# Row maxima one step ahead, the row of shifts carried by VectorE transposition and small transfers, and other splits of the keys

## The chip, the cores and the metric

The kernel runs on one core of a Trainium2 chip. A core has five engines that take their own instructions in order and wait for each other by semaphores: TensorE (PE; its weight loads are listed as PEld), VectorE (DVE), ScalarE (ACT), GpSimd (POOL) and SyncE (SP), which issues the transfers here. The metric is device time in microseconds; lower is better.

## The reference

Routed attention, followed by a feed-forward block. A query sees only the keys whose nearest centroid is its own:

```python
batch, n_heads, seq, head_dim = (4, 8, 768, 64);  n_clusters = 16
q_assign = np.argmax(np.einsum('bhsd,hcd->bhsc', q_n, c_n), axis=-1)
k_assign = np.argmax(np.einsum('bhsd,hcd->bhsc', k_n, c_n), axis=-1)
mask = q_assign[:, :, :, None] == k_assign[:, :, None, :]
scores = scale * np.matmul(q, k.transpose(0, 1, 3, 2))
scores = np.where(mask, scores, -1000000000.0)
scores = scores - np.max(scores, axis=-1, keepdims=True)
attn = np.exp(scores)
attn = attn / (np.sum(attn, axis=-1, keepdims=True) + 1e-09)
out = np.matmul(attn, v)
...
h = x @ w_in                       # 3072 tokens, 512 -> 2048
sp = np.maximum(h, 0.0) + np.log1p(np.exp(-np.abs(h)))
g = h * erf(sp)
return g @ w_out                   # 2048 -> 512
```

## The kernel before, in words

The kernel has two stages. The first is attention, some 380 us of the span; the second, the feed-forward block, is not touched. Every engine's instructions of the first stage stand in the order in which the code issues them (`keep_in_program_order`), SP's transfers through `queues[0]` too; the stores to `x_dram` in `divide` are the exception (`nc.sync` directly).

Attention goes by 16 **pairs** of heads. The two heads e = 0, 1 of a pair lie on partitions 0 to 63 and 64 to 127. A pair has two halves of 384 queries and six blocks of 128 keys, so 12 units; a **period** (`period(p, i)`, i = 0 to 5) handles two units: periods 0 to 2 the first half, 3 to 5 the second. The exponentials need a shift for each query, its maximum over the allowed keys, before the half begins, so the maxima of a half are worked out beforehand:

- `maxima_step` forms, for 128 queries (block t) and a part of the keys, the products with queries on the partitions: a first pass over bf16 copies of q and k (`qv`, `kv`) and a second over the rows of the masks (`qm`, `km`), both into the one tile `wide`, which VectorE reduces (`nmx`). TensorE can't write `wide` again before that reduction is done. Each block t has two steps, the first with `KEYS[t]` keys and the second with the rest of the 768.
- Each period has two such steps, half a pair ahead of the scores. The **open step** stands at the period's head, both passes on their own. The **shared step** has its first pass after the period's products q k (`products`, tile `sc`, f32) and its second pass between the two `scores`, which add mask and shift to `sc`; those use 32 of the 64 partitions of each head, the shared step's second pass the other 32.
- When three blocks are through, VectorE takes the smaller of the negated maxima of both parts into `lowest`. At the head of the next period 0 or 3 comes the **turn** (`turn`): six products with `lowest` as weights bring the values into rows of the tile `turned`, and ScalarE copies one row for each head into `qm` (rows 0 and 64), as the row of shifts.

After the scores of a period come, on TensorE: a mask product or the similarities where the period has one; `attend`, 32 products with v for the two units of the period before; and in periods 0 and 3 the sums of `divide`, eight products over the tile that GpSimd has accumulated (`accumulate`, `more_out`). Attend and sums write to `turned`, as similarities and masks do.

The other engines, in the order that the code gives:

- ScalarE: the exponentials (`curve`, two per period, `pr<-sc`), mask copies into `qm` and `km`, logarithm and exponential of the sums (`inv`), and passes over weight strips, which arrive as 64-bit words: in periods 0 and 3 the **sign pass** (`x_own<-x_own`, to int16) behind the two exponentials and ahead of `inv`. In pairs 1 to 14 there is one in period 3.
- VectorE: reductions, 32x32 transpositions (`qT`, `kT`, `sims`, `hotT`, `aside`), in period 0 the copy of the mask into `km`, the division (`den`, then two operations on `turned`, then `x`), two operations on a weight strip.
- GpSimd: in periods 1 and 4 the add that completes a strip (`summed`; the next strip's fetch is issued behind it), then the accumulation of `pr`.

The similarities of pair p + 2 (q and k with the centroids, eight products in the profile) stand in period 3 behind the scores. Of the four mask products for pair p + 1, `MASKS` names period and place: (0, 2) k first half, (2, 3) q first half, (2, 2) k second half, (5, 2) q second half; place 2 is behind the second scores, and its copy on ScalarE stands between the two exponentials except in period 0, where VectorE makes it before the shared step's reduction.

Of the kernel before, what the change touches and what calls it, by code (L numbers as in the profile page):

```python
# [10 lines left out]
BF16 = mybir.dt.bfloat16  # L11
# [16 lines left out]
TW = QW + 1  # L28
HJ = NJ // 2
HP = H // 2  # L30
KEYS = (256, 256, 352, 384, 256, 352)
NPAIR = B * HP
DM, DFF = H * D, 2048
NFT = DFF // P
# [13 lines left out]
N_LATE = 4  # L48
PLACE_OF = [n % 5 for n in range(25)] + [2, 3, 2]
LAST_X = 11  # L50
MASKS = {(0, 2): ("k", 0), (2, 3): ("q", 0), (2, 2): ("k", 1), (5, 2): ("q", 1)}
FIRST_MASKS = {(2, 0): ("k", 0), (2, 1): ("q", 0), (2, 2): ("k", 1), (5, 2): ("q", 1)}

KAPPA = {1: (0, 1), 2: (0, 0), 0: (1, 1), 3: (1, 0)}
HOME = {0: 4, 1: 0, 2: 2, 6: 3, 4: 1, 5: 5}
# [76 lines left out]
def kernel(  # L132
# [55 lines left out]

    lowest = [const.tile([P, HJ, P], BF16, name=f"lowest{i}") for i in range(2)]
    maxima = [const.tile([P, 2, NJ, 3], F32, name=f"nmx{i}") for i in range(2)]  # L190


    lows = [
# [140 lines left out]
    ve.tensor_copy(out=identb, in_=ident)  # L334
    ve.memset(minus, -1.0)
    ve.memset(alleps, S * EPS)
    for t in lowest:
        ge.memset(t, 0.0)

    cn = setup[:, D : 3 * D].rearrange("p (e d) -> p e d", e=2)  # L340
# [104 lines left out]

    turns = []

    def maxima_step(p, i, sm=wide, behind=False):

        st = pairs[p]  # L450
        nmx = maxima[p % 2]
        t, half = divmod(i, 2)

        first = KEYS[t]
        keys = (slice(0, first), slice(first, S))[half]
        n = keys.stop - keys.start

        def passes(a, b, start, rows):
            for e in range(2):
                r = slice(e * D + rows.start, e * D + rows.stop)  # L460
                te.matmul(
                    sm[:, e, 0:n], lhsT=st[a][r, t * P : (t + 1) * P],
                    rhs=st[b][r, keys], start=start, stop=not start,
                )

        passes("qv", "kv", True, slice(0, D))
        if behind:
            yield
        passes("qm", "km", False, slice(Q, D) if behind else slice(0, D))
        if behind:  # L470
            yield
        ve.tensor_reduce(
            out=nmx[:, :, t, half], in_=sm[:, :, 0:n], axis=AX.X, op=ALU.max, negate=True
        )
# [89 lines left out]
    def divide(u):  # L564

        p, half, _ = units[u]
        st = pairs[p]
        av = st["av", half]

        psum = turned[1 - half][:, 0:QW]  # L570
        for g in range(4):
            te.matmul(psum[g * Q : (g + 1) * Q], lhsT=minus, rhs=st["acc", half][:, g], start=True, stop=True)

        if u + 1 < len(units):
            inv = routep.tile([P, QW], F32, name="inv")
            den = routep.tile([P, QW], F32, name="den")
        else:
            inv, den = part_of(0, 4 * HW, QW), part_of(1, 0, QW)
        ae.activation(out=inv, in_=psum, func=ACT.Ln, bias=alleps, scale=-1.0)
        ae.activation(out=inv, in_=inv, func=ACT.Exp, scale=-1.0)  # L580
        yield
        ve.scalar_tensor_tensor(
            out=den, in0=psum, scalar=S * EPS, in1=inv, op0=ALU.subtract, op1=ALU.mult
        )
        for k in range(2):
            raw = av[:, k, 0:QW]
            ve.scalar_tensor_tensor(
                out=raw, in0=raw, scalar=av[:, k, QW : QW + 1], in1=inv, op0=ALU.add, op1=ALU.mult
            )
            if k == 0:  # L590
                yield
        x = part_of(0, (2 * p + half) % 4 * HW, HW).rearrange("p (k x) -> p k x", k=2)
        ve.scalar_tensor_tensor(
            out=x, in0=den.unsqueeze(1).to_broadcast([P, 2, QW]), scalar=2.0, in1=av[:, :, 0:QW],
            op0=ALU.add, op1=ALU.mult,
        )
        b, r = divmod(p, HP)
        for g in range(4):
            rows_of, at = r * P + g // 2 * D, b * S + half * HW + g % 2 * QW
            nc.sync.dma_start(  # L600
                out=x_dram[rows_of : rows_of + D, at : at + QW].rearrange("(k r) x -> r k x", k=2),
                in_=x[g * Q : (g + 1) * Q],
            )
        if half == 1:
            del pairs[p]
        yield
# [725 lines left out]
    def period(p, i):  # L1332
        u = 2 * NJ * p + 2 * i
        n1, n2 = 2 * p - 1, 2 * p
        early = lambda n: 0 <= n < N_EARLY

        def mask(place):
            which = (MASKS if p else FIRST_MASKS).get((i, place))
            if which:
                return masks(p + 1, *which, turned[0 if i in (0, 5) else 1], place == 2, ve if i == 0 else ae)  # L1340
            return lambda: None

        if u > 0:
# [20 lines left out]
        rows = D if u == 0 or u + NJ >= len(units) else Q  # L1364
# [12 lines left out]
        if i == 3:  # L1377
            similarities(p + 2)
            routing[0] = choose(p + 2, turned[0], True)
        curve(u)  # L1380
        later()
        curve(u + 1)
        if u == 0:
            step_ahead(1)
            similarities(1)
            routing[0] = choose(1, turned[0])
            next(routing[0])
            next(routing[0])
            vectors(1, "q")
            vectors(1, "k")  # L1390
        if i == 0 and early(n1 - 1):
            bounded(n1 - 1)
            shifted(n1 - 1)
            sign(n1 - 1)
        elif i == 1 and early(n1):
            size_and_rest(n1)
        elif i == 3 and early(n1):
            sign(n1)
        elif i == 5 and early(n2):
            rest(n2)  # L1400
        for _ in range(min(len(forms), FORMS.get(p, {}).get(i, 0))):
            forms.pop(0)[0]()
        if i == 3:
            next(routing[0], None)
# [79 lines left out]
    for n in range(len(places) - 1):  # L1484
        fetch(n)
    for i in range(NJ):
        run(maxima_step(0, i, also if i % 2 else wide))
# [4 lines left out]
    step_ahead(0)  # L1492
    warm(2, turned[0], zeros)
    turn(0, 0, (ae.copy, ve.tensor_copy))
    turns.clear()
# [111 lines left out]
```

## Time and profile before

| what | us |
|---|---|
| median of 3 runs (953.5 to 954.16) | 953.59 |
| the profiled execution | 953.27 |
| its span | 951.6 |
| TensorE busy in the span | 942.7 (99%) |
| VectorE busy | 789.8 (83%) |
| ScalarE busy | 556.4 (58%) |
| GpSimd busy | 504.3 (53%) |

The profile is of one execution. Nearly every row names line 123, the helper through which instructions are recorded, so rows are told apart by their tiles: `wide` and `nmx` belong to the maxima, `sc` to products and scores, `pr` to the exponentials, `turned<-identb,lowest` to the turn, `turned<-pr,in_v` to attend, `turned<-more_out,minus` to the sums of the division. An f32 product shows as two instructions. Busy times of neighbouring products overlap, and the distance from one start to the next is what a step takes. The steady periods repeat from pair to pair within a few hundredths of a microsecond; the pair from 200 to 224 us, whose period 4 begins at 204.72, stands for all.

### The profile page before, as it was taken

What the parts mean: (1) busy time and instruction counts of PE and PEld (TensorE: products, weight loads), DVE (VectorE), ACT (ScalarE), POOL (GpSimd) and SP (SyncE); (2) the same over time, 40 slices, a digit from 0 to 9 for tenths busy, and PEclk for the clock granted to TensorE, in tenths of its full rate; (3) what the DMA queues carried; (4) which work ended last, traced back from release to release, by engine and by line L of the source; (5) the groups of instructions that cost most, each with busy time, mean ns of one, the idle gap of its engine ahead of it and who ended that gap; (6) DMA issues with size and microseconds to landing.
All of it is one profiled execution on the core that took longest, in us unless ns stands there. A gap on an engine that the chain in (4) does not pass through costs nothing.

```text
span 951.6 us, 22455 instructions
## 1 busy us (share of the span) xinstructions
PE 942.7 (99%) x8938; PEld 719.8 (76%) x8938; DVE 789.8 (83%) x1402; ACT 556.4 (58%) x854; POOL 504.3 (53%) x355
## 2 busy tenths in 40 slices
PE   8999999999999999999999999999999999999998
PEld 3555555555555555588888888998999899989987
DVE  8888888888888887888886688688868977897887
ACT  3777777887777777566513642654257236525541
POOL 1688888888888888899109211360064016103600
PEclk9999999999999999999999999999999999999999
DMA  9355555555454522032786247353444436343533
GB/s 214 73 113 113 113 112 104 120 112 104 103 117 84 132 59 58 18 120 111 199 250 237 101 103 201 127 191 111 155 146 154 133 111 211 111 155 123 155 112 111
DMA packets 175385, 123.14 MB, mean 129 GB/s; under 512 B 131632, under 2 KB 142384, under 8 KB 175280
## 3 DMA queue, kind: packets, MB, share of 16 engines
q1 hardware_dynamic: 170912, 116.29, 43.4%
q0 software_dynamic: 1872, 4.98, 2.9%
q8 instruction: 71, 1.16, 0.5%
q10 hardware_dynamic: 2496, 0.43, 0.2%
q14 instruction: 34, 0.28, 0.1%
HBM read 91.78 MB, written 23.33 MB: 121 GB/s over the span
## 4 chain that ended last, share of the span: by engine, by line
PE 93%; DVE 2%; ACT 1%; issue 1%; DMA 1%; POOL 1%; SPq 0%; DVEq 0%; ACTq 0%; POOLq 0%
PE bank L123 40%; PE turned L123 31%; PE sc L123 17%; PE wide L123 6%; DVE g L123 1%; POOL more_out L123 1%; ACT a_s L123 0%; DMA g_more<-in_moe_w_out_dram 0%; DVE nmx L123 0%; DMA in_k<-in_k_dram 0%; ACT L123 0%; SPq L123 0%; DVE kT L123 0%; ACT osb L123 0%; ACT w_out L123 0%
## 5 line engine op out<-in xcount | busy, mean ns | idle before, releaser
L123 POOL TENSOR_TENSOR more_out<-more_out,pr 128x768 f32<-128x768 f32 x128 | 217.2, 1697 | 15.9 <-ACT pr L123 6.5
L123 DVE TENSOR_REDUCE nmx<-wide 128x2 f32<-128x1024 f32 (+2 forms) x189 | 179.4, 949 | 40.3 <-PE wide L123 39.3
L123 ACT ACTIVATE pr<-sc 128x768 f32<-128x768 f32 x192 | 148.7, 810 | 79.9 <-PE wide L123 66.0
L123 PE MATMUL turned<-pr,in_v 128*32 128x193 f32 x3072 | 144.8, 330 | 0.0
L123 POOL TENSOR_TENSOR g<-g 128x512 f32<-128x512 f32 x36 | 47.2, 1311 | 180.7 <-DVE g L123 178.8
L123 PEld LDWEIGHTS turned<-pr,in_v 128*32 128x32 f32 x3072 | 91.5, 109 | 51.0 <-issue 21.9
L123 DVE TENSOR_TENSOR g<-g 128x512 f32<-128x512 f32 x132 | 90.7, 687 | 22.5 <-PE bank L123 11.4
L123 PE MATMUL sc<-qT,kT 64*128 64x384 f32 x528 | 98.3, 485 | 0.0
L123 DVE TENSOR_TENSOR g<-bank,g 128x256 f32<-128x256 f32 (+1 forms) x128 | 64.6, 530 | 16.1 <-PE bank L123 9.5
L123 PE MATMUL bank<-g_more,g 128*128 128x256 f32 x320 | 75.6, 379 | 0.0
L123 PE MATMUL bank<-x_own,w_in 128*128 128x128 f32 (+1 forms) x440 | 74.0, 310 | 0.0
L123 ACT ACTIVATE a_s<-g 128x1024 f32<-128x1024 f32 x38 | 39.5, 1054 | 56.9 <-POOL g L123 45.3
L123 POOL TENSOR_TENSOR more_out<-pr,pr 128x768 f32<-128x768 f32 x32 | 58.9, 1842 | 20.2 <-ACT pr L123 20.2
L123 DVE TENSOR_TENSOR g<-a_s,g 128x512 f32<-128x512 f32 x76 | 67.3, 904 | 0.4 <-ACT a_s L123 0.4
L123 PEld LDWEIGHTS bank<-g_more,g 128*128 128x128 f32 x320 | 60.8, 190 | 8.3
L123 PEld LDWEIGHTS bank<-x_own,w_in 128*128 128x128 f32 x440 | 63.1, 191 | 4.6 <-issue 0.6
L123 PE MATMUL wide<-kv,qv 64*128 64x512 bf16 (+2 forms) x378 | 64.9, 327 | 1.0 <-ACT km L123 0.6
L123 PE MATMUL bank<-w_out,g 128*128 128x256 f32 x280 | 64.5, 379 | 0.0
L123 PE MATMUL wide<-km,qm 32*128 32x512 bf16 (+2 forms) x378 | 62.4, 326 | 0.0
L123 ACT ACT_TABLE_LOAD x40 | 51.3, 1283 | 18.3 <-DVE g L123 17.7
L123 PEld LDWEIGHTS sc<-qT,kT 64*128 64x128 f32 x528 | 47.8, 187 | 18.6 <-issue 0.9
L123 PEld LDWEIGHTS <-qv 64*128 64x128 bf16 x384 | 24.6, 93 | 47.1 <-issue 29.6
(239 smaller groups left out, 2030.4 us busy)
## 6 DMA issues: line engine op xcount, KB each, us to landing
g_more<-b_dram SPq DMA_DIRECT2D x52, 512.0 KB, 3.3
g_more<-w_dram SPq DMA_DIRECT2D x84, 256.0 KB, 2.9
x_own<-in_moe_w_in_dram SPq DMA_DIRECT2D x13, 512.0 KB, 5.4
in_v<-in_v_dram SPq DMA_DIRECT2D x32, 192.0 KB, 3.2
x_dram<-more_out SPq DMA_DIRECT2D x128, 48.0 KB, 1.7
x_own<-x_dram SPq DMA_DIRECT2D x6, 1024.0 KB, 5.8
in_k<-in_k_dram SPq DMA_DIRECT2D x59, 96.0 KB, 2.8
in_q<-in_q_dram SPq DMA_DIRECT2D x58, 96.0 KB, 5.0
```

What stands on the lines that cost most here:

```text
L123: ins = getattr(self.engine, name)(*args, **kw)
```

## The change

- **Steps.** The maxima run one step further ahead: of the twelve steps of a pair the open places now hold the second parts and the shared places the first parts. `KEYS` becomes 384 for block 0 and 512 for the others, so an open step has 256 keys (384 once) and a shared one 512 (384 once). To get ahead, pair 1's first half is done in five joined steps (`JOINED`) in pair 0's periods 3 to 5; the half before them keeps the old splits.
- **Row of shifts.** For all but pair 0's halves, VectorE reduces into two columns of a tile `least`, transposes its 32x32 blocks into `least_rows`, and four transfers from SP's queue, each of 2 partitions x 3 x 32 values of bf16, bring the rows into `qm`. This is issued right behind the last reduction of the half, an open step's (period 2 for the second half, period 5 for the next pair's first), in place of the turn's six products and two copies.
- **Moves.** From pair 1 on, the similarities of pair p + 2 and the transposition of their result stand at the head of period 3, before the open step. The q mask of the second half goes from place 2 of period 5 to place 2 of period 3. The transposition of k for pair p + 2, with the loads behind it, goes from the end of period 2 to right behind its open step.
- **Stores.** The stores to `x_dram` go a place later and stand in SP's order.

```diff
-KEYS = (256, 256, 352, 384, 256, 352)
+KEYS = (384, 512, 512, 512, 512, 512)
+FIRST_KEYS = (256, 256, 352, 384, 256, 352)
+JOINED = (
+    ((0, 0, 0, 512),), ((0, 1, 512, 768), (1, 0, 0, 256)), ((1, 1, 256, 768),), ((2, 0, 0, 512),), ((2, 1, 512, 768),),
+)
-MASKS = {(0, 2): ("k", 0), (2, 3): ("q", 0), (2, 2): ("k", 1), (5, 2): ("q", 1)}
-FIRST_MASKS = {(2, 0): ("k", 0), (2, 1): ("q", 0), (2, 2): ("k", 1), (5, 2): ("q", 1)}
+MASKS = {(0, 2): ("k", 0), (2, 3): ("q", 0), (2, 2): ("k", 1), (3, 2): ("q", 1)}
+FIRST_MASKS = {(2, 0): ("k", 0), (2, 1): ("q", 0), (2, 2): ("k", 1), (5, 3): ("q", 1)}
...
+    def pieces_of(i, keys_of):
+        t, part = divmod(i, 2)
+        return ((t, part, *((0, keys_of[t]), (keys_of[t], S))[part]),)
+
-    def maxima_step(p, i, sm=wide, behind=False):
+    def maxima_step(p, pieces, sm=wide, behind=False, by_products=False):
...
-        ve.tensor_reduce(
-            out=nmx[:, :, t, half], in_=sm[:, :, 0:n], axis=AX.X, op=ALU.max, negate=True
-        )
-        if i in (NJ - 1, 2 * NJ - 1):
-            h = i // NJ
-            ve.tensor_reduce(
-                out=lowest[h][:, :, ::D].rearrange("p t e -> p e t"),
-                in_=nmx[:, :, h * HJ : (h + 1) * HJ], axis=AX.X, op=ALU.min,
-            )
-            turns.append((p, h))
+        at = 0
+        for t, part, lo, hi in pieces:
+            ve.tensor_reduce(
+                out=nmx[:, :, t, part], in_=sm[:, :, at : at + hi - lo], axis=AX.X, op=ALU.max, negate=True
+            )
+            at += hi - lo
+        h, last = divmod(t, HJ)
+        if part and last == HJ - 1:
+            of_half = nmx[:, :, h * HJ : (h + 1) * HJ]
+            if by_products:
+                ve.tensor_reduce(
+                    out=lowest[h][:, :, ::D].rearrange("p t e -> p e t"), in_=of_half, axis=AX.X, op=ALU.min,
+                )
+                turns.append((p, h))
+            else:
+                into_rows(p, h, of_half)
+
+    def into_rows(p, h, of_half):
+
+        st = pairs[p]
+        ve.tensor_reduce(
+            out=least[h][:, :, 0:2].rearrange("p t e -> p e t"), in_=of_half, axis=AX.X, op=ALU.min
+        )
+        ve.transpose(out=least_rows[h].rearrange("p t q -> p (t q)"), in_=least[h].rearrange("p t q -> p (t q)"))
+        row = st["qm"][::D, h * HW : (h + 1) * HW].rearrange("e (t b q) -> e t b q", t=HJ, q=Q)
+        for b in range(P // Q):
+            queues[0].dma_start(out=row[:, :, b], in_=least_rows[h][b * Q : b * Q + 2])
+        st["shift", h] = True
...
+        yield
         b, r = divmod(p, HP)
         for g in range(4):
...
-            nc.sync.dma_start(
+            queues[0].dma_start(
...
-    def step_ahead(u, behind=False):
-        p, i = divmod(u + NJ, 2 * NJ)
-        steps = maxima_step(p, i, behind=behind) if p < NPAIR else iter(())
+    def step_ahead(p, i, behind=False):
+        if p == 0 and i < NJ:
+            steps = maxima_step(0, pieces_of(NJ + i, FIRST_KEYS), behind=behind, by_products=True)
+        elif p == 0 and i < NJ + len(JOINED):
+            steps = maxima_step(1, JOINED[i - NJ], behind=behind)
+        else:
+            p, i = divmod(2 * NJ * p + NJ + 1 + i, 2 * NJ)
+            steps = maxima_step(p, pieces_of(i, KEYS), behind=behind) if p < NPAIR else iter(())
...
             for which in turns if i in (0, 3) else ():
                 turn(*which)
                 turns.remove(which)
-            step_ahead(u)
+            if i == 3 and p:
+                similarities(p + 2)
+                routing[0] = choose(p + 2, turned[0], True)
+                next(routing[0], None)
+            step_ahead(p, 2 * i)
+            if i == 2:
+                transposes(p + 2, "k")
...
-        second = step_ahead(u + 1, True) if u > 0 else iter(())
+        second = step_ahead(p, 2 * i + 1, True) if u > 0 else iter(())
...
-        if i == 3:
+        if i == 3 and not p:
             similarities(p + 2)
             routing[0] = choose(p + 2, turned[0], True)
...
-        elif i == 2:
-            transposes(p + 2, "k")
```

More of the change, by code (lines that the diff above doesn't have):

```diff
@@ L190 @@
     maxima = [const.tile([P, 2, NJ, 3], F32, name=f"nmx{i}") for i in range(2)]
+    least = [const.tile([P, HJ, Q], BF16, name=f"least{i}") for i in range(2)]
+    least_rows = [const.tile([P, HJ, Q], BF16, name=f"least_rows{i}") for i in range(2)]
     lows = [
@@ L336 @@
     ve.memset(alleps, S * EPS)
-    for t in lowest:
+    for t in lowest + least:
         ge.memset(t, 0.0)
@@ L446 @@
     turns = []
-    def maxima_step(p, i, sm=wide, behind=False):
+    def pieces_of(i, keys_of):
+        t, part = divmod(i, 2)
+        return ((t, part, *((0, keys_of[t]), (keys_of[t], S))[part]),)
+    def maxima_step(p, pieces, sm=wide, behind=False, by_products=False):
         st = pairs[p]
         nmx = maxima[p % 2]
[L452 to L456, printed above, removed]
+        total = sum(hi - lo for _, _, lo, hi in pieces)
         def passes(a, b, start, rows):
[L459 to L463, printed above, removed]
-                )
+            at = 0
+            for t, _, lo, hi in pieces:
+                for e in range(2):
+                    r = slice(e * D + rows.start, e * D + rows.stop)
+                    te.matmul(
+                        sm[:, e, at : at + hi - lo], lhsT=st[a][r, t * P : (t + 1) * P],
+                        rhs=st[b][r, lo:hi], start=start and at == 0, stop=not start and hi - lo + at == total,
+                        skip_group_check=len(pieces) > 1,
+                    )
+                at += hi - lo
         passes("qv", "kv", True, slice(0, D))
@@ L1361, in period @@
         mask(1)()
-        second = step_ahead(u + 1, True) if u > 0 else iter(())
+        second = step_ahead(p, 2 * i + 1, True) if u > 0 else iter(())
         next(second, None)
-        rows = D if u == 0 or u + NJ >= len(units) else Q
+        rows = D if u == 0 or u + NJ + 2 >= len(units) else Q
         scores(u, rows)
@@ L1383, in period @@
         if u == 0:
-            step_ahead(1)
+            step_ahead(0, 1)
             similarities(1)
@@ L1403, in period @@
         if i == 3:
-            next(routing[0], None)
+            if not p:
+                next(routing[0], None)
             if early(n1):
@@ L1486 @@
     for i in range(NJ):
-        run(maxima_step(0, i, also if i % 2 else wide))
+        run(maxima_step(0, pieces_of(i, FIRST_KEYS), also if i % 2 else wide, by_products=True))
         if i == 1:
@@ L1491 @@
             warm(2, turned[0], zeros)
-    step_ahead(0)
+    step_ahead(0, 0)
     warm(2, turned[0], zeros)
```

2 lines of the change are left out of this document (added).

## The prediction

> **What bounds the kernel now.** I read the page's head and chain of waits first, then the busy time of the attention stage as one window.
>
> ```profile
> span 951.6 us, 22455 instructions
> ...
> PE 93%; DVE 2%; ACT 1%; issue 1%; DMA 1%; POOL 1%; SPq 0%; DVEq 0%; ACTq 0%; POOLq 0%
> ```
> ```profile
> 30.70:394.00 363.30, 363.30 (x5281) 204.65 (x5279) 308.93 (x499) 283.94 (x458) 303.18 (x188) 1.00 0.44 97
> ```
>
> The chain is TensorE nearly everywhere, at full granted clock. VectorE is busy 308.93 of 363.30 us and GpSimd 303.18, so both have only some 15% to spare: a delay there can reach TensorE. The change lies in this stage, so next came the timeline of one pair, engine by engine, TensorE first. Columns: start, busy time, engine, operation.
>
> ```profile
> 201.88 0.34 PE L123 MATMUL sc<-qm,km 32*128 32x384 bf16 x2
> ...
> 204.28 0.51 PE L123 MATMUL turned<-more_out,minus 128*32 128x192 f32 x8
> 204.72 0.28 PE L123 MATMUL wide<-kv,qv 64*128 64x256 bf16 x2
> ...
> 204.95 1.46 PE L123 MATMUL sc<-qT,kT 64*128 64x384 f32 x8
> 206.25 0.38 PE L123 MATMUL wide<-kv,qv 64*128 64x512 bf16 x2
> 206.56 0.34 PE L123 MATMUL sc<-qm,km 32*128 32x384 bf16 x2
> ...
> 206.99 1.51 PE L123 MATMUL turned<-pr,in_v 128*32 128x193 f32 x32
> 208.43 0.32 PE L123 MATMUL wide<-kv,qv 64*128 64x352 bf16 x2
> ...
> 210.75 1.51 PE L123 MATMUL turned<-pr,in_v 128*32 128x193 f32 x32
> 212.08 0.34 PE L123 MATMUL turned<-identb,lowest 128*32 128x128 bf16 x6
> 212.35 0.34 PE L123 MATMUL wide<-kv,qv 64*128 64x384 bf16 x2
> ...
> 212.69 1.45 PE L123 MATMUL sc<-more_out 64*128 64x384 f32 x8
> 213.98 0.33 PE L123 MATMUL wide<-kv,qv 64*128 64x384 bf16 x2
> 214.24 0.34 PE L123 MATMUL sc<-qm,km 32*128 32x384 bf16 x2
> ...
> 214.67 1.51 PE L123 MATMUL turned<-pr,in_v 128*32 128x193 f32 x32
> 216.00 0.51 PE L123 MATMUL turned<-more_out,minus 128*32 128x192 f32 x8
> ```
>
> Distances between starts count here, since busy times overlap. Period 4 of this pair begins at 204.72, period 5 at 208.43, period 0 at 212.35: one product follows the next with no hole, so every product taken away is a gain until some other engine is late. How close are the others? First VectorE:
>
> ```profile
> 205.19 0.68 DVE L123 TENSOR_REDUCE nmx<-wide 128x2 f32<-128x512 f32 x1
> ...
> 206.25 0.35 DVE L123 SCALAR_TENSOR_TENSOR den<-turned,inv 128x192 f32<-128x192 f32 x1
> 206.51 0.42 DVE L123 SCALAR_TENSOR_TENSOR turned<-turned,inv 128x192 f32<-128x192 f32 x1
> 206.99 1.23 DVE L123 TENSOR_REDUCE nmx<-wide 128x2 f32<-128x1024 f32 x1
> ...
> 209.06 0.89 DVE L123 TENSOR_REDUCE nmx<-wide 128x2 f32<-128x704 f32 x1
> ...
> 211.78 0.18 DVE L123 TENSOR_REDUCE lowest<-nmx 128x6 bf16<-128x18 f32 x1
> ...
> 213.77 0.57 DVE L123 STREAM_TRANSPOSE hotT<-hot 128x384 bf16<-128x384 bf16 x1
> 214.88 0.62 DVE L123 TENSOR_SCALAR km<-turned,nbig 128x384 bf16<-128x384 f32 x1 [0.55 <-PE turned L123]
> 215.42 0.95 DVE L123 TENSOR_REDUCE nmx<-wide 128x2 f32<-128x768 f32 x1
> ```
>
> Here the reduction at the end of period 0 ends at 215.42 + 0.95 = 216.37, and TensorE wants its tile back for the next step 0.44 after 216.00, at 216.44: 0.07 us to spare. It stands behind the copy of `km`, which itself waited 0.55 us for TensorE's mask product.
>
> ```profile
> 202.34 1.51 ACT L123 ACTIVATE pr<-sc 128x768 f32<-128x768 f32 x2 [1.10 <-PE wide L123]
> 203.74 1.38 ACT L123 ACTIVATE x_own<-x_own 128x512 int16<-128x512 f32 x1
> ...
> 205.31 0.36 ACT L123 ACTIVATE inv<-inv 128x192 f32<-128x192 f32 x1
> ```
> ```profile
> 211.44 0.48 ACT L123 ACTIVATE qm<-turned 128x384 bf16<-128x384 f32 x1
> 211.82 0.82 ACT L123 ACTIVATE pr<-sc 128x768 f32<-128x768 f32 x1
> ```
> ```profile
> 205.20 1.29 POOL L123 TENSOR_TENSOR w_in<-w_in,x_own 128x512 int32<-128x512 int32 x1 [1.73 <-ACT x_own L123]
> ...
> 208.37 6.98 POOL L123 TENSOR_TENSOR more_out<-more_out,pr 128x768 f32<-128x768 f32 x4
> ```
>
> And here is a chain across three engines: ScalarE's sign pass of a weight strip ends at 203.74 + 1.38 = 205.12; GpSimd, idle for 1.73 us until then, starts its add at 205.20 and then works until 208.37 + 6.98 = 215.35; TensorE reads that result in the sums at 216.00. There are 0.65 us to spare.
>
> **The change, part by part.** *The turn goes.* From the attend products to the next open step are 1.44 us without a turn (206.99 to 208.43) and 1.60 with one (210.75 to 212.35). The six products themselves seem to take 0.27 (212.08 to 212.35), but 0.11 of it is the change of tile shape, paid either way. So 0.16 each; 30 turns fall away (two in each pair from 1 on, while pair 0 keeps its own): -4.8 us. ScalarE's two copies cost nothing before: ScalarE waited 1.10 us for TensorE behind them.
>
> *Other key splits.* An open step of 256 keys takes 0.23 (204.72 to 204.95), one of 384 takes 0.34 (212.35 to 212.69), so 352 about 0.31. A pair had 256, 256, 352, 384, 256, 352 (1.65) and gets 384 and five times 256 (1.49). The first pass of the shared step takes 0.31 for 512 keys (206.25 to 206.56) and 0.26 for 384 (213.98 to 214.24), 416 about 0.27: 1.73 becomes 1.81. Its second pass is free, because scores to attend take 0.43 beside 512 keys (206.56 to 206.99) as beside 384 (214.24 to 214.67). Net -0.08 in each of 14 pairs: -1.1.
>
> *Similarities to the head of period 3.* The same eight products; the change of shape moves with them. On VectorE their transposition (0.57, as `hotT`) now precedes the reduction of 384 keys (about 0.95): 0.2 + 0.57 + 0.95 = 1.72 after they end, where TensorE returns for the tile after 0.11 + 0.34 + 1.29 = 1.74. Between 0 and 0.07 per pair, taken as 0.03: +0.4.
>
> *The q mask to period 3.* The product hides beside the scores, but its copy on ScalarE now stands between the two exponentials and ahead of the sign pass. It delays what follows by 0.37 (211.44 to 211.82). Before, the sign pass ended 3.24 after the scores at 201.88; now 3.61. At the same time the similarities no longer lie between scores and period 4, which begins 0.43 + 1.33 (210.75 to 212.08) + 0.44 (204.28 to 204.72) = 2.20 after the scores instead of 2.84. Against TensorE the sign pass thus ends 1.40 into period 4 instead of 0.40: **1.0 us later**. Two engines wait for it.
>
> VectorE: the inverse (205.31 + 0.36 = 205.67) ends 0.55 after the sign pass, so `den` starts 2.0 into period 4 instead of 1.53, the next operation ends 0.26 + 0.42 later at 2.68, the reduction of 512 keys at 2.60 + 1.23 = 3.83 (neighbours overlap by 0.08, as 206.25 + 0.35 does with 206.51), and with 0.05 to pass it on (an estimate; from 216.37 to 216.44 it was at most 0.07) period 5 starts at 3.88 instead of 3.71: +0.17. Bounds 0 and 0.25. Behind that reduction VectorE's queue holds the rest of the division and period 5's reduction.
>
> GpSimd: it starts at 1.48 and, with 10.15 us of unbroken work, ends 11.63 into period 4's clock. TensorE comes to the sums at 3.88 + 3.71 (period 5) + 0.23 + 1.29 + 0.31 + 0.43 + 1.33 = 11.18. With 0.06 to pass it on it waits **0.51** in period 0, and the sums, the next open step and VectorE's work on it wait with it. GpSimd's end is fixed by its start, so 0.17 and 0.51 make 0.68 together even if the first is smaller. Bounds for the 0.51: 0.25 (the next item's wait alone) and 0.65.
>
> *512 keys in period 0's shared step.* `km` starts 0.21 after the attend products, which begin 2.27 into period 0; so `km` runs 2.48 to 3.10, the reduction (1.23 instead of 0.95) 3.02 to 4.25, and the next open step can start at 4.30 where TensorE alone would be there at 4.04. These 0.26 lie under the 0.51: the larger counts, not the sum. Without GpSimd's lateness they stand alone.
>
> *The row of shifts by transposition and transfers.*
>
> ```profile
> 209.18 1.72 SPq L600 DMA_DIRECT2D x_dram<-more_out  x4
> ```
> ```profile
> x_own<-in_moe_w_out_dram SPq DMA_DIRECT2D x9, 512.0 KB, 3.9
> x_dram<-more_out SPq DMA_DIRECT2D x66, 48.0 KB, 1.7
> ...
> in_q<-in_q_dram SPq DMA_DIRECT2D x24, 96.0 KB, 5.0
> ```
>
> (Second view: the transfers by kind from 200 to 400 us, size and median us from issue to landing.)
>
> In period 5 the open step's reduction began 0.63 in (209.06 against 208.43); now about 0.79, by the 0.17 above. Then 0.68 (256 keys), 0.18, and a transposition of 96 columns: at most 0.57, the price of 384, at least 0.14, a quarter of it; I take 0.3. The row is ready about 2.0 in. Four issues at 0.43 (1.72 over 4), the last 1.3 later, landing after 1.7: 5.0, at worst 5.3. It is read at 3.71 + 0.23 + 1.29 + 0.31 = 5.54, hence hidden; up to 0.25 of a delay would still lie under the 0.51. For the other half the similarities add 0.67 of slack or more. The issues go ahead of the loads of q and k and of the stores to `x_dram`, which have a period or more to spare; VectorE's transpositions fall into periods 2 and 5. In period 5 the queue runs 0.79 + 0.68 + 0.18 + 0.3 + 0.57 (the transposition of `hot`) + 1.23 = 3.75 less some 0.13 of overlap, in time for 3.71; at 0.57 for the new one it would be 0.2 late, again under the 0.51. Nothing for it. The Trainium skill, page "DMA: Bandwidth & Descriptors", section "Anatomy of one DMA", speaks against small transfers: a fixed cost of about 2.0 us each, most of it the receipt (the page's fit is for transfers that GpSimd starts). The stores here land in 1.7; by the page the last transfer would land 0.3 later, still in time, and the sum would be the same.
>
> *The ends.* Pair 0's joined steps put 512 keys twice where 256 stood (some 0.2 each), the last pair loses a shared step (-0.3), pair 1's period 0 has the 0.26 alone: together +0.35.
>
> Sum: -4.8 - 1.1 + 0.4 + 14 x (0.17 + 0.51) + 0.35 = **+4.4 us**. The profiled execution took 953.27 us (its span is 951.6), so 957.6; the median of the runs, 953.59, lies 0.3 above, so 957.9.
>
> **The rivals.** *GpSimd has cover* (its add starts sooner, or the sums are not the first to wait): then only 0.26 counts in period 0, 14 x 0.25 = 3.5 less, 954.4, no change. For it: 0.65 us to spare before. Against it: GpSimd runs from its add to 215.35 without a hole, and its idle 1.73 names the sign pass.
>
> *ScalarE is not late* (faster). If the copy of the mask and the sign pass end no more than 0.5 later against TensorE, neither VectorE in period 4 nor GpSimd in period 0 waits; only the 0.26 behind `km` is left: -4.8 - 1.1 + 0.4 + 14 x 0.26 + 0.35 = -1.5, and without that wait as well -5.1. So 952.1 down to 948.5. For it: ScalarE sheds two copies for each half. Against it: those lay in idle time, and the order on ScalarE is fixed.
>
> *The shift arrives late.* Loads of q are issued right behind the weight fetch and take 5.0 us to land, not 1.7. If the shift's transfers shared that lot they would land 3.3 later, so 2.5 behind what the 0.51 and the margin cover: 14 x 2.5 = 35 more, about 993. The same skill page ("Queues, rings and completion order") has it that each DMA engine takes descriptors in ring order; the 5.0 agrees. Against it: period 4's fetch leaves after GpSimd's add, 2.8 into that period, and with 3.9 to land it is through 2.8 into period 5, before the last shift transfer is issued.
>
> *The products stay in the steady pairs.* Then the 4.8 is missing and the copies remain on ScalarE: 962 or more. The diff calls the turn only for pair 0.
>
> **How the numbers follow.** Chances: forecast 0.58; GpSimd has cover 0.17; ScalarE not late 0.15; shift late or turns kept 0.10. The time is the forecast's, 957.8. Its own bounds are 955 (0.35 for 0.51) and 960.5 (0.65, and 0.07 for 0.03). The low end goes to 952 to take in the cover case, the high end to 961; the two outer cases are left out in part. What a measurement can tell from no change is 0.2%, 1.9 us: faster is 0.11 (most of ScalarE not late), same 0.21 (cover and the rest of it), slower 0.68.
>
> **What would show it.** TensorE should wait for GpSimd's `more_out` ahead of the sums in period 0 of pairs 2 to 15, about half a microsecond each; `den` should start 2.0 into period 4; GpSimd's idle time ahead of its add in period 4 should rise from 1.7 to about 2.8; attend to open step should be 1.44 wherever a turn stood. The forecast is wrong if periods 0 and 4 last no longer than 4.1 and 3.75, or if scores wait for a transfer.

## The result, and the profile after

The changed kernel takes 963.27 us (median of 4 runs, 963.21 to 963.38) beside 953.55 for the kernel before on the same chip: 1.0101 times as long, 95% interval 1.0089 to 1.0114. It is slower, as forecast, but by 9.7 us instead of 4.3. From here on, times of kernels other than these two are compared with the kernel before in the same series, which had medians of 953.5 to 953.6.

The page's head and its chain of waits, after:

```profile
span 961.5 us, 22306 instructions
...
PE 75%; DVE 11%; ACT 4%; DMA 3%; SPq 3%; issue 2%; POOL 2%; DVEq 0%; ACTq 0%; POOLq 0%
```

TensorE had 93% of this chain and now has 75%; VectorE went from 2% to 11%. The span grew by 9.9 us. To see where, take the distances between the starts of the open steps, period by period, as the prediction did. The table is worked out from the traces' start times (means over the pairs named, us); 0 to 5 are the periods.

| kernel, pairs | 0 | 1 | 2 | 3 | 4 | 5 | a pair |
|---|---|---|---|---|---|---|---|
| before, 2 to 7 | 4.09 | 3.71 | 4.08 | 4.69 | 3.71 | 3.92 | 24.19 |
| before, 8 to 12 | 4.09 | 3.73 | 4.08 | 4.68 | 3.71 | 3.92 | 24.21 |
| after, 2 to 7 | 4.36 | 3.71 | 4.49 | 4.27 | 3.76 | 3.92 | 24.51 |
| after, 8 to 12 | 4.36 | **4.32** | 4.49 | 4.27 | 3.77 | 3.92 | 25.12 |

The early pairs cost 0.32 more each, close to the 0.29 of the forecast (4.4 us less 0.35 for the ends, over 14). From pair 8 on something else adds 0.59, all of it in period 1. Summed over the whole span: the steady loss, 13 pairs, 4.1; period 1 of pairs 8 to 14, 3.9; pair 0 from period 3 on, 0.9; one longer period 5 in pair 13, 0.4; pair 14's other periods and what follows them, 0.4; and 0.2 by which pair 0's first open step came later, which differs as much between runs of kernels that share that part (12.06 to 12.37 us).

First a steady pair, as in the prediction. TensorE from period 4 (207.98) to the open step of period 1 (220.04), then the three engines behind it. Columns: start, busy time, engine, operation, and in brackets idle time with what ended it.

```profile
207.98 0.28 PE L127 MATMUL wide<-kv,qv 64*128 64x256 bf16 x2
...
211.75 0.29 PE L127 MATMUL wide<-kv,qv 64*128 64x256 bf16 x2
...
214.03 1.51 PE L127 MATMUL turned<-pr,in_v 128*32 128x193 f32 x32
215.66 0.29 PE L127 MATMUL wide<-kv,qv 64*128 64x256 bf16 x2
...
218.06 1.51 PE L127 MATMUL turned<-pr,in_v 128*32 128x193 f32 x32
219.57 0.53 PE L127 MATMUL turned<-more_out,minus 128*32 128x192 f32 x8
220.04 0.28 PE L127 MATMUL wide<-kv,qv 64*128 64x256 bf16 x2
```
```profile
207.93 1.35 ACT L127 ACTIVATE x_own<-x_own 128x512 int16<-128x512 f32 x1
```
```profile
209.36 1.30 POOL L127 TENSOR_TENSOR w_in<-w_in,x_own 128x512 int32<-128x512 int32 x1 [2.91 <-ACT x_own L127]
...
212.55 6.97 POOL L127 TENSOR_TENSOR more_out<-more_out,pr 128x768 f32<-128x768 f32 x4
```
```profile
209.87 0.36 DVE L127 SCALAR_TENSOR_TENSOR den<-turned,inv 128x192 f32<-128x192 f32 x1 [0.17 <-ACT inv L127]
...
213.25 0.18 DVE L127 TENSOR_REDUCE least<-nmx 128x6 bf16<-128x18 f32 x1
213.47 0.28 DVE L127 STREAM_TRANSPOSE least_rows<-least 128x96 bf16<-128x96 bf16 x1
213.78 0.57 DVE L127 STREAM_TRANSPOSE aside<-hot 32x384 bf16<-32x384 bf16 x1
214.38 1.23 DVE L127 TENSOR_REDUCE nmx<-wide 128x2 f32<-128x1024 f32 x1
```

The chain across three engines is there: the sign pass ends 207.93 + 1.35 = 209.28, 1.30 into period 4 (forecast 1.40, before 0.40); GpSimd idles 2.91 until it (forecast 2.8); it works until 212.55 + 6.97 = 219.52; the sums start 0.05 later. They come 219.57 - 218.06 = 1.51 after attend instead of 1.33, a wait of 0.18, not 0.51. The rest of GpSimd's lateness had been spent in front of it: in period 5 TensorE takes 215.66 - 214.03 = 1.63 from attend to the open step instead of 1.44, because VectorE's reduction ends at 214.38 + 1.23 = 215.61. The small transposition takes 0.28 (I took 0.3), but these four operations do not overlap by the 0.13 that I took off.

Now the late pairs, 8 to 14. This is the chain of waits after, 241 to 250 us, in order of time (start, length, what), through the end of period 0 and period 1 of pair 9:

```profile
243.32 0.62 DVE km L127
243.93 1.13 DVE nmx L127
245.07 1.09 DVE w_out L127
...
246.18 0.43 DVE w_out L127
246.61 0.61 DVE nmx L127
...
247.27 0.39 PE wide L127 x2
```

Two operations on a strip of weights stand in the path: VectorE must finish them before the open step's reduction, and TensorE's shared step waits for that. They stood in the queue before as well. What differs is how long the first takes. VectorE and GpSimd, after:

```profile
244.98 1.63 DVE L127 TENSOR_SCALAR w_out<-w_out 128x512 f32<-128x512 f32 x2
...
244.59 1.28 POOL L127 TENSOR_TENSOR more_in<-more_in,w_in 128x512 f32<-128x512 f32 x1
```

and before:

```profile
264.70 1.05 DVE L123 TENSOR_SCALAR w_out<-w_out 128x512 f32<-128x512 f32 x2
...
263.72 1.29 POOL L123 TENSOR_TENSOR w_in<-w_in 128x512 f32<-128x512 f32 x1
```

The two operations take 1.63 together instead of 1.05, and beside them GpSimd makes a left form of the weights: a sum or difference of two blocks of weights for the feed-forward stage, which `POOL_FORMS` gives it in period 1 from pair 8 on. Before, the form was nearly done when VectorE came (it ends at 265.01); after, it had just begun (ends 245.87). In both traces VectorE's first operation ends 0.28 after the form's end. That suggests a lock, not a slower pace, and the experiments test it.

### The profile page after: what moved, and what is told of

Same layout as the page of the kernel before. It is cut to its first block, busy times and chain, and to the rows that moved or that the text cites. A ratio compares the mean times of both kernels' runs of the same rounds, so it can differ in the third digit from the quotient of the medians.

```text
span 961.5 us, 22306 instructions
## 1 busy us (share of the span) xinstructions
PE 947.2 (99%) x8758; PEld 711.7 (74%) x8758; DVE 800.3 (83%) x1432; ACT 530.6 (55%) x794; POOL 504.5 (52%) x357
## 4 chain that ended last, share of the span: by engine, by line
PE 75%; DVE 11%; ACT 4%; DMA 3%; SPq 3%; issue 2%; POOL 2%; DVEq 0%; ACTq 0%; POOLq 0%
PE bank L127 42%; PE turned L127 21%; PE sc L127 9%; DVE nmx L127 5%; PE wide L127 4%; SPq L127 3%; DMA in_q<-in_q_dram 2%; ACT x_own L127 2%; POOL more_out L127 1%; ACT pr L127 1%; DVE w_out L127 1%; DMA x_own<-in_moe_w_out_dram 1%; ACT qm L127 1%; DVE turned L127 1%; DVE more_out L127 1%
## 5 line engine op out<-in xcount | busy, mean ns | idle before, releaser
L127 DVE TENSOR_REDUCE nmx<-wide 128x2 f32<-128x512 f32 (+2 forms) x189 | 178.3, 944 | 23.0 <-PE wide L127 22.5
L127 PEld LDWEIGHTS <-qv 64*128 64x128 bf16 x384 | 27.1, 93 | 68.5 <-issue 53.4
L127 PE MATMUL wide<-kv,qv 64*128 64x256 bf16 (+2 forms) x378 | 65.4, 327 | 6.0 <-DVE nmx L127 3.7
L127 PE MATMUL wide<-km,qm 64*128 64x256 bf16 (+4 forms) x378 | 62.7, 326 | 0.0
```

Of the source, the lines that this page charges most:

```text
L127: ins = getattr(self.engine, name)(*args, **kw)
```

## The experiments

The first theory: the loss comes from the late sign pass, which makes GpSimd late against TensorE, and in the late pairs the form then holds up VectorE. Rivals: the form's own length, the mask's copy on ScalarE, or the transfers.

**The form a period later.**

```diff
-POOL_FORMS = {p: (1,) for p in range(8, 16)}
+POOL_FORMS = {p: (2,) for p in range(8, 16)}
```

> The changed kernel with one edit: from pair 8 on, GpSimd makes its form of the weights in period 2 instead of period 1. Theory (lock): in period 1 VectorE's first operation on a weight strip can't start before GpSimd's form ends, and the form is late because GpSimd is; so with the form elsewhere that operation falls from about 1.17 us to about 0.42, period 1 of the late pairs from 4.31 to about 3.72, and the time from 963.3 by 7 x 0.58 = 4.1 to about 959. Rival (the operation is slow for another reason, such as its strip's own data or place in VectorE's queue): period 1 stays at 4.3 and the time within 0.5 of 963.3. Second rival (GpSimd is merely late for something else): the 0.6 us shows up again in period 2 or 3.

959.46 us (1.0061, 1.0046 to 1.0076). Period 1 of the late pairs is 3.71 again. So the 0.6 hangs on the form's place beside VectorE's operation. Some 0.1 of it came back: period 3 rose to 4.39, and in pair 14 to 5.11, where the sums waited for GpSimd.

**The sign pass a period earlier.**

```diff
-        elif i == 3 and early(n1):
+        elif i == 2 and early(n1):
             sign(n1)
```

> The changed kernel with one edit: in pairs 1 to 14 ScalarE's sign pass of period 3 stands at the end of period 2, where ScalarE has time until the scores of period 3. Theory (chain from ScalarE over GpSimd): GpSimd's add in period 4 starts over 2 us sooner, the sums of period 0 no longer wait (attend to sums 1.33 instead of 1.50), period 4 falls from 3.76 to about 3.71, and the form of the late pairs is over before VectorE comes to its strip, so period 1 falls from 4.31 to 3.71. VectorE's own lateness in periods 5 (3.92) and 0 (4.3) stays. Together about 1.4 + 4.2 less: 957.5. Rival (VectorE alone sets the pace; GpSimd's lateness is a result): less than 1 us is gained, and period 1 stays at 4.3.

955.05 us (1.0015, 1.0006 to 1.0025): the best single edit, 8.2 of the 9.7 us. Periods 4 and 1 are back at 3.71, in late pairs too; period 5 is 3.76 and period 0 is 4.31. VectorE and GpSimd at the same place of pair 9:

```profile
242.00 0.88 DVE L127 TENSOR_SCALAR w_out<-w_out 128x512 f32<-128x512 f32 x2
...
240.77 1.29 POOL L127 TENSOR_TENSOR more_in<-more_in,w_in 128x512 f32<-128x512 f32 x1
```

The form ends at 242.06, 0.06 after VectorE has begun, and the pair of operations takes its shortest time, 0.88. I had expected more to remain.

**The mask's copy back in period 5.**

```diff
-MASKS = {..., (2, 2): ("k", 1), (3, 2): ("q", 1)}
+MASKS = {..., (2, 2): ("k", 1), (5, 3): ("q", 1)}
```

> The changed kernel with one part undone as far as the order allows: the q mask of the second half is formed in period 5 again, between the two units' products, so its copy on ScalarE leaves period 3. Theory: the sign pass comes 0.37 us sooner, GpSimd with it; the mask's 0.16 on TensorE in period 5 is hidden by VectorE's lateness there; the wait of the sums (0.17) goes, and the form collides for 0.37 less in the late pairs: 14 x 0.1 + 7 x 0.37, about 4 less, so 959.5. Rival (it is the move of the similarities alone that makes ScalarE late): the mask's copy counts for nothing, and the time is 963 to 965.

958.55 us (1.0051, 1.0035 to 1.0068). Period 4 is back at 3.71, but period 1 of the late pairs is still 4.24. The sign pass of pair 7, on ScalarE:

```profile
205.98 1.35 ACT L127 ACTIVATE x_own<-x_own 128x512 int16<-128x512 f32 x1
```

It ends at 207.33, and period 4 starts at 206.34 in this run: 0.99 into it, against 1.30 after and 0.40 before. So the mask's copy makes VectorE's wait in period 4, but only a third of the lateness. The rest comes from the other part that the prediction named: the similarities left the stretch between scores and period 4, so TensorE is there 0.6 sooner (2.26 after the scores in the changed kernel, 2.84 before). A run further down, with the products kept and the sign pass in period 3, has the similarities back behind the scores as well: there the sign pass of pair 7 ends at 208.12, 0.39 into period 4 (207.73), as before the change.

**The row of shifts by transfers alone, in the kernel before.** The new into_rows takes the turn's place from pair 1 on; steps, splits, mask and similarities stay. The stores to `x_dram` go one place later in the queue.

```diff
             h = i // NJ
+            if p:
+                into_rows(p, h, nmx[:, :, h * HJ : (h + 1) * HJ])
+                return
```

> The kernel before with one part of the change alone: from pair 1 on the row of shifts comes by VectorE transposition and four transfers instead of the turn; steps, keys, similarities and masks as before. Theory (the row takes 0.5 from reduction to transposition, 4 issues at 0.5 and 1.5 to land, so about 3.7 us, and here its last reduction ends 0.4 us before the period does): the scores of periods 0 and 3 wait about 1.3 us in each of 30 halves, less 0.16 each for the turn: 953.5 + 34, about 988. That would show that the step sooner is what pays for the transfers. Rival (the transfers hide under the period's head anyway): 949 to 954.

999.56 us (1.0479, 1.0463 to 1.0495). That is much more than the 988 expected. From the waits of this run between 60 and 400 us (engine, what it waited for, us in total, times, longest):

```profile
PE sc L123 <- DMA qm<-least_rows: 34.3, 26, 1.5
```

Scores wait for the row in each half, and periods 0 and 3 last 1.5 to 1.6 longer, where 1.3 was expected. Periods 2 and 5, from whose ends a turn is gone, fall by the prediction's 0.16 each (3.92 and 3.76). In the changed kernel TensorE's products have such a wait once, 0.26 in the last half of the last pair (403.98), where no steps for a next pair lie ahead of the scores. So the transfers are hidden only because the maxima come a step sooner: the two parts need each other.

The second theory, on what is left after the sign pass: VectorE's queue is over-full in periods 5 and 0, by the small transposition and by the 512 keys behind `km`. The next four all start from the run with the sign pass earlier.

**384 instead of 512 keys in the shared step of period 0.**

```diff
-KEYS = (384, 512, 512, 512, 512, 512)
+KEYS = (384, 512, 512, 512, 384, 512)
```

> The sign pass a period earlier, as in the run of that name, and of the second key split 384 instead of 512 in the shared step of period 0 (the open step of period 1 gets 384 instead of 256). Theory (what is left of the wait in period 0 is VectorE's reduction of 512 keys behind km, which ends 4.26 into the period): that reduction becomes 0.95 and ends at 4.0, period 0 falls from 4.31 to 4.17, period 1 rises by 0.1 for the longer open step, so -0.04 in each of 14 pairs, 954.5 us. Rival (the sums wait for GpSimd): period 0 stays at 4.31 and period 1 still rises by 0.1: 956.5.

954.91 us (1.0014, 1.0005 to 1.0022). In pairs 2 to 7 period 0 falls to 4.06, more than expected, and period 1 rises to 3.81 as expected: 24.10 a pair instead of 24.25. Yet the total barely moves, for in the late pairs period 1 lasts 4.03. VectorE and GpSimd there:

```profile
241.15 1.15 DVE L127 TENSOR_SCALAR w_out<-w_out 128x512 f32<-128x512 f32 x2
...
240.27 1.28 POOL L127 TENSOR_TENSOR more_in<-more_in,w_in 128x512 f32<-128x512 f32 x1
```

A faster period 0 brought VectorE to the strip earlier, while the form was at work again: 1.15, between 0.88 and 1.63. In the four traces shown, VectorE began 0.98, 0.39, 1.23 and 0.88 after the form (before, after, sign pass earlier, this one), and the two operations took 1.05, 1.63, 0.88 and 1.15. Begin and length add up to 2.02 to 2.03 in the three cases where VectorE was really held, which is one fixed point after the form's start: VectorE gets through only when the form, of 1.28 to 1.29, has ended. The rest of the traces agree: in all 13, VectorE's strip operation began beside a form 63 times up to pair 14. In the 57 where 0.14 or more of the form was left, it ended 0.28 to 0.29 after the form; in the six with less than 0.1 left, it took its usual 0.42. A slower pace would have no such fixed end; this is a lock. The Trainium skill, page "SBUF — State Buffer", section "Who interferes with whom", has this rule: VectorE in its two-port modes, which `tensor_scalar` can enter, and GpSimd share one port pair, and the one that comes second is blocked for the whole of the other's instruction. These traces agree with it.

**The transposition into `aside` in period 0.** Its call in period 5 is taken out, and period 0, which runs what is left of the routing, does it there ahead of `hotT`.

```diff
-        if i == 5:
-            next(routing[0], None)
```

> The sign pass a period earlier, and the transposition into aside moved from period 5 to period 0, in front of that into hotT. Theory (VectorE is over-full in period 5 by the new transposition of 96 columns): period 5 falls from 3.758 to 3.71, the open step's reduction of period 0 starts 0.77 instead of 0.88 into it and TensorE's 0.08 before the shared step's first pass goes; the wait behind km stays. 0.1 x 14 less, 953.6 us. Rival (period 5 is long for another reason, such as the transfers' issue): no change, 955.0; or, if the mask product of period 0 now waits for aside, 956.

953.11 us (0.9995, 0.9986 to 1.0004). Period 5 falls to 3.71 and period 0 to 4.23, as expected. So the small transposition, for which the prediction had "Nothing", had a price of some 0.05 in period 5 and 0.08 at its echo in period 0, where VectorE was late for the open step.

**VectorE eased further.** On top of that, ScalarE copies `km` in period 0 between the two exponentials, and the sign pass of that period moves into period 5 of the pair before.

```diff
-                return masks(p + 1, *which, turned[...], place == 2, ve if i == 0 else ae)
+                return masks(p + 1, *which, turned[...], place == 2)
...
-            sign(n1 - 1)
...
             rest(n2)
+            sign(n2)
```

> On top of aside in period 0: the copy of km in period 0 by ScalarE between the two exponentials instead of by VectorE, and the sign pass of period 0 moved into period 5 of the pair before. Theory (VectorE's queue in periods 5 and 0 is all that is left of the loss in the steady pairs): the reduction of 512 keys in period 0 ends 3.5 to 3.7 into it instead of 4.26, period 0 falls from 4.31 to 4.2, and with 3.71 in period 5 that is 0.16 to 0.2 per pair against the run with only the sign pass moved: 952.3 us. Rival (ScalarE becomes late in period 5 or 0 instead): 955 or more.

952.17 us (0.9986, 0.9977 to 0.9995). Period 0 is 4.16. VectorE now reduces the 512 keys well before the end of period 0. Its next operations run into the form again, but are early enough that period 1 stays at 3.71 to 3.76 in pairs 8 to 14.

**And 512 keys in the first split.**

```diff
-KEYS = (384, 512, 512, 512, 512, 512)
+KEYS = (512, 512, 512, 512, 512, 512)
```

> The run before, and the first key split 512 instead of 384: the open step of period 3 gets 256 keys, the shared step of period 2 512. Theory: the open step is 0.1 shorter by the same rows as in the prediction (0.23 against 0.34) and the shared step's reduction ends 3.9 into a period of 4.5, so -0.1 in each of 14 pairs: 950.9 us. Rival (VectorE late in period 2 or 3): the 0.1 comes back there, 952.3.

950.89 us (0.9970, 0.9959 to 0.9982), the fastest of all: 2.6 us under the kernel before. Period 3 fell by 0.18 to 4.09, period 2 rose by 0.08. VectorE and GpSimd are hardly in TensorE's way any more, though the lock still holds the strip here (VectorE, pair 8):

```profile
215.11 1.56 DVE L127 TENSOR_SCALAR w_in<-w_in 128x512 f32<-128x512 f32 x2
```

The strip took 1.56 us, nearly as long as in the changed kernel, but began 0.66 ahead of the next open step (215.77) and not 0.17 ahead of it (244.98 to 245.15): the lock costs only where VectorE is next on the path.

**The products kept for every pair.** The run with the sign pass earlier, but the row of shifts by TensorE and ScalarE throughout, the similarities back at the end of period 3 and the mask back in period 5.

```diff
-            steps = maxima_step(p, pieces_of(i, KEYS), behind=behind) if ...
+            steps = maxima_step(p, pieces_of(i, KEYS), behind=behind, by_products=True) if ...
```

> The sign pass a period earlier, but the row of shifts made by TensorE's products and ScalarE's copies for every pair as before, and for that the similarities back at the end of period 3 and the q mask back in period 5; so of the change only the steps made sooner, the key splits and the joined steps of pair 0 are left. Theory (the turn costs TensorE 0.16 each, 30 times, and moving the similarities and the mask costs some 0.06 in period 3): the turns give back 4.8, the moves give 0.06 x 14 and the small transposition in period 5 (0.05) is gone: 955.0 + 4.8 - 1.5 = 958.3 us. Rival (a turn hides beside other work and its removal was worth nothing): 953.5 or less.

965.88 us (1.0128, 1.0111 to 1.0145). This run was confounded: the turn's copies on ScalarE came late behind the sign pass, and the scores of period 3 waited 0.50 (period 3 lasted 5.28, and 4.78 without that wait in the next run). So it says nothing on the turn, and was run again with the sign pass in period 3, as before:

> As the run with the products kept for every pair, but with the sign pass back in period 3, where the kernel before has it: in the run before this one the sign pass in period 2 stood on ScalarE ahead of the turn's copies, and the scores of period 3 waited 0.73 for them. Theory: without that wait the steady pair lasts 25.01 - 0.73 = 24.28, 965.9 - 14 x 0.73 = 955.7 us, so that sooner steps, splits and joined steps alone lose 2 us and the row by transfers, with the moves that go with it, gains next to nothing over the turns (955.0 with the sign pass early). Rival (a turn is worth 4.8 in the whole as in the rows): 958.3 or more.

958.59 us (1.0055, 1.0041 to 1.0068). My expectation here fell: I had misread the wait as 0.73, and the rival was right. A pair lasts 24.51. The run with transfers and an early sign pass has 24.25, 0.27 less (3.5 us in the whole). The turn's own rows say the same: attend to open step is 1.60 with a turn and 1.45 without. Without the transfers, the change as it stands in this run costs 5 us over the kernel before; 3 of them are period 0 with its 512 keys behind `km` (4.30 instead of 4.09, 14 times).

**The joined step a period later in pair 0**, on the fastest run; open steps of periods 3 to 5 take 256, 512, 512 keys instead of 512, 512, 256.

```diff
-    ((0, 0, 0, 512),), ((0, 1, 512, 768), (1, 0, 0, 256)), ((1, 1, 256, 768),), ((2, 0, 0, 512),), ...
+    ((0, 0, 0, 256),), ((0, 1, 256, 768),), ((1, 0, 0, 512),), ((1, 1, 512, 768), (2, 0, 0, 256)), ...
```

> The run with the split of 512, and in pair 0 the joined step in the shared step of period 4 instead of period 3, so that the open steps of periods 3, 4 and 5 take 256, 512 and 512 keys instead of 512, 512 and 256. Theory (an open step of 512 keys costs TensorE 0.2 and the wait for VectorE's reduction another 0.2): period 3 falls from 5.11 to 4.68, period 5 rises from 3.99 to 4.4, sum unchanged: 950.9 us. Rival (period 3 is long because the joined shared step has two reductions): periods 3 and 5 both near their time in the steady pairs, 950.4.

951.00 us (0.9973, 0.9963 to 0.9982), no change, as expected. Period 3 falls to 4.68, and periods 5 and 0 get it back (4.26 and, in pair 1, 4.36). The price goes with the 512 keys of an open step. In the changed kernel, pair 0, period 3, TensorE and VectorE:

```profile
30.90 0.39 PE L127 MATMUL wide<-kv,qv 64*128 64x512 bf16 x2
31.13 0.38 PE L127 MATMUL wide<-km,qm 64*128 64x512 bf16 x2
31.34 1.45 PE L127 MATMUL sc<-qT,kT 64*128 64x384 f32 x8
32.83 0.39 PE L127 MATMUL wide<-kv,qv 64*128 64x256 bf16 x4
```
```profile
31.55 1.23 DVE L127 TENSOR_REDUCE nmx<-wide 128x2 f32<-128x1024 f32 x1 [1.13 <-PE wide L127]
```

The open step takes 0.44 instead of 0.23, and then TensorE wants the tile back 1.29 after 31.34, at 32.63, while VectorE's reduction ends at 32.78: 0.41 in all, of which the prediction had "some 0.2".

## Why the prediction was right and wrong

*The turn*: right. 0.16 in the rows and at the ends of periods 2 and 5 of the run with the row of shifts alone; in the whole 3.5 us instead of 4.8 in the run that keeps the products, where the moves that go with the transfers count against them.

*Key splits, similarities, mask*: about right in sum. Left out was that a mask product beside a shared step of 512 keys costs TensorE 0.05: in periods 0 and 3 it starts 0.06 after the last scores, where it was 0.01 to 0.02 beside 384 and 416 keys (and is 0.01 again in the run with 384 in period 0). The similarities' move costs 0.06 in period 3 (1.35 instead of 1.29 from the products to the shared step), at the upper end of the 0 to 0.07 given.

*Period 4's wait*: right in kind, sized 0.17, measured 0.06. The sign pass ended 0.1 sooner than worked out, and VectorE with it. With the mask's copy back it is gone, as the step said.

*The shift by transfers*: right that they are hidden, but for one wait of 0.26 in the last pair, and right that this hangs on the sooner maxima. One price was off, 0.59 for an issue (2.36 for the four in period 5, the row below) instead of 0.43, within the slack there was.

```profile
213.81 2.36 SPq L127 DMA_DIRECT2D qm<-least_rows  x4
```

*"Nothing for it"*, on VectorE's queue in period 5: wrong. It was counted as "in time", with 0.13 of overlap; there is none, and period 5 loses 0.19 (0.05 with the sign pass early).

*GpSimd's 0.51 in period 0*: the size was off there (0.18), but the total up to the sums was nearly right, for the reason the step gave: GpSimd's end is fixed by its start, and a wait ahead of it only takes from it. TensorE comes to the sums 11.59 after the start of period 4; without any wait it would be 11.01 by the prediction's own steps, so 0.58 instead of 0.68, and the 0.1 is what the sign pass ended sooner. That the pair as a whole came out as close as 0.32 beside 0.29 is partly luck: these 0.1 too much stand against about as much that was left out in period 3.

*The step that failed* is this one about GpSimd, where it follows GpSimd's work to its end: "GpSimd: it starts at 1.48 and, with 10.15 us of unbroken work, ends 11.63 into period 4's clock." It stops at the sums. It does not ask what GpSimd does next, and on whom that falls. From pair 8 on, GpSimd goes straight to a left form, now half a microsecond later against TensorE, and so on top of VectorE's strip operation: 3.9 us in period 1 of pairs 8 to 14. No term of the sum held it, and no rival either. With the form elsewhere the same kernel takes 959.46, inside the range of the prediction. The profile before had it in view: the same operation took 0.38 to 0.59 there, the long ones where the form ran beside it.

```profile
L123 DVE TENSOR_SCALAR w_out<-w_out x24: 382/427/590, 240.5 to 373.4; 128x512 f32<-128x512 f32 x12, 128x512 uint32<-128x512 uint32 x12
```

(Before, one tile's operations on VectorE: least, median and largest ns.) After, the largest is 1183.

*The ends*: sized +0.35, measured about 0.9 for pair 0 alone. The 0.4 for two open steps of 512 keys left out the wait for VectorE's reduction behind each, another 0.2 twice.

Of the rivals, "GpSimd has cover" and "ScalarE is not late" both fell as descriptions of this kernel. With the sign pass moved, the second became true, and the time went to 955.05, not to the 952.1 or less that the rival gave: VectorE's waits in periods 5 and 0 and pair 0 make the difference. What stays open is the longer period 5 of pair 13 (4.28, where VectorE's transposition started 0.39 late); it was not tried by itself, but is gone in the runs with `aside` in period 0.

## What to carry to other kernels

When a change delays an engine, follow it past the first wait, to everything that it does next, and lay the other engines' queues beside it. An operation whose time varies between its occurrences (0.38 to 0.59 here) marks a collision that is already there and can grow. A part that speeds up one engine may need its slack elsewhere: the same change that lost 9.7 us gained 2.6 when two sign passes, one transposition, one copy and one key split were moved to where their engines had room.

## What the runs showed of the hardware

VectorE's `tensor_scalar` on 128x512 f32 in SBUF (alone 0.42) and GpSimd's `tensor_tensor` (1.28) do not run together: where VectorE's comes second and has to wait, it ends 0.28 to 0.29 after GpSimd's, whenever it began, and lasts up to 1.2. The profile counts this as busy time of VectorE, not as a wait. It holds the other way round too. In pair 15 of the kernel before, GpSimd's form begins while a VectorE operation on tiles in SBUF is at work, and takes 1.72 instead of 1.28:

```profile
384.38 0.92 DVE L123 TENSOR_TENSOR more_in<-w_in,more_in 128x512 f32<-128x512 f32 x1
...
384.71 1.72 POOL L123 TENSOR_TENSOR more_in<-w_in 128x512 f32<-128x512 f32 x1
```

A 32x32-block transposition of 96 bf16 columns on VectorE takes 0.28 where 384 take 0.57, and it does not overlap with its neighbours (0.03 to 0.04 lie between them). A transfer of 0.4 KB from SBUF to SBUF costs SyncE's queue 0.50 to 0.72 to issue; where scores did wait for the last of four (403.98), they began 1.5 after its issue had started (402.45).
